# Idle-time identity products on the tensor engine, and a new order of the first loads, in a fused attention and expert kernel

## The chip, the cores and the metric

The kernel runs on one core of one Trainium2 chip. The metric is the device time of one execution in microseconds (us). Before the change it is 997.39 us, the median of three runs.

The core has five engines that run their own instruction queues: PE (the tensor engine), DVE (vector), ACT (scalar), POOL (GpSimd) and SP, which here only issues DMAs. ACT issues a few DMAs too. An instruction waits on semaphores for work of other engines; behind it on its own engine everything waits with it.

## The reference

Top-k style attention (scores within `tau` of the row's maximum survive) feeds a mixture of four experts. Sizes: 4 batches, 8 heads, 576 positions of 64; the 2304 x 512 result goes through experts with 1024 hidden units each.

```
scores = scale * q @ k.T                       # (4, 8, 576, 576)
thresh = max(scores, -1) - tau
scores = where(scores >= thresh, scores, -1e9)
attn   = softmax(scores)
x      = (attn @ v)  as (2304, 512)
p      = domain_probs / sum(domain_probs)
out    = sum over e of  p[:, e] * (relu(x @ w1[e]) @ w2[e])
```

All inputs are float32.

## The kernel before

The kernel describes its work as operations with an engine, a guessed duration, the tiles that they use, and a priority. `Plan.schedule` then runs a list scheduler over them: it walks a model of the five engines in time, and whenever an engine is free it takes the ready operation of lowest priority number. `Plan.emit` issues the instructions in the order that came out. So a change in a guessed time can move instructions on every engine; the durations themselves are not used by the chip. `Plan.clock` stretches the guessed duration of a PE operation when the model believes the tensor engine's clock to be low.

Heads are treated in pairs. The first batch (b = 0) runs in float32, the other three with split float16 operands. For a pair of heads in the first batch:

- `t_load` loads q and k (four DMAs of 128 KB, the first 512 positions); `tails` loads the last 64 positions of all heads of the batch into one tile `tl` (two 64 KB DMAs of k, one 128 KB DMA of q);
- `t_prep` transposes q and k on PE against the identity `ident` into the PSUM tile S (or its twin S0 for odd pairs): eight transposes of `raw` (line 628), two of `tl` (632, 633). ACT copies the result to T (647);
- `item` makes scores: `emit_qk` (919, 925) writes S in PSUM, DVE reads it into SS and takes the row extreme (978, two instructions, one per head), ACT takes the exponential (1001), DVE masks it and sums (1010); PE transposes E into ET (1030, 1059), ACT copies to PT (941);
- `group` multiplies with v (PE `av`, 1242 and 1251), spreads the row sums over columns (PE `rp`, 1206; ACT `rb`, 1226), multiplies the two on DVE (1273) and splits the result into two float16 halves X (ACT 1287, DVE 1295).

Then come the experts. `unit` does experts 0 and 1 while attention still runs (first layer 1358, second layer 1400, `mm` tiles in PSUM; ACT makes `hr` and `h`, 1370 and 1378); `unit7` does experts 2 and 3 afterwards (1594, 1674). Weights are scaled and split first (ACT 453 squares, PE 463 sums into S, then ACT 826 and DVE 851).

[...] Columns 0 to 575 and 960 to 1535 hold scores; between them lie two small places `am0` and `am1` for the sums of line 463.

DMA issues of SP and ACT share eight completion semaphores (`DMAHW0` to `DMAHW7`), which are handed out round the list; a DMA that takes a semaphore over waits at issue until the one before on it has landed.

Of the kernel before, what the change touches and what calls it, by code (L numbers as in the profile page):

```python
# [21 lines left out]
class Plan:  # L22
# [14 lines left out]
    GAP, FILL = 400, 3000  # L37
    WINDOW, WARMUP = 3413.0, 4000.0
    warm, cold, work, window, pe_end = True, 0.0, 1e9, 0, 0.0
    FREED, LANES = 55, 8  # L40
    START, DONE, HELD = 625, 1000, 877

    def __init__(self):
        self.ops, self.writer, self.readers = [], {}, {}
        self.slots, self.kinds, self.order, self.users = {}, {}, {}, {}
        self.tiles, self.loose = {}, set()
# [39 lines left out]
    def clock(self, now, ns, use):  # L86
        if use[0][0] != "mm" and self.warm:
            return ns
        self.warm = False
        w = int(now / self.WINDOW)  # L90
        if w != self.window:
            if self.work < 0.4 * self.WINDOW or w > self.window + 1:
                self.cold = self.WARMUP
            self.window, self.work = w, 0.0
        if now - self.pe_end > 300 and self.cold > 0:
            self.cold = self.WARMUP
        if self.cold > 0:
            slow = min(ns, self.cold / 2)
            self.cold -= 2 * slow
            ns += slow  # L100
        self.work += ns
        self.pe_end = now + ns
        return ns

    def schedule(self):
# [21 lines left out]
        starts, self.plan = [], {}  # L127
# [19 lines left out]
        while True:  # L147
            progress = True
            while progress:
                progress = False  # L150
                for e in engines:
# [13 lines left out]
                    if pick is None:  # L165
                        continue
# [10 lines left out]
                    if e == "PE":  # L177
                        ns = self.clock(now, ns, use)
                    end = now + ns + (self.TAIL[e] if e == "PE" else 0)
                    free[e] = end - self.TAIL[e]  # L180
                    if xfer and e != "SP":
                        dma = max(dma, end + self.START) + xfer
                        end = dma + self.DONE
                    elif xfer:
                        dma = max(dma, end + self.START) + abs(xfer)
                        if xfer < 0:
                            free[e] = max(end, dma - min(self.HELD, 100 - xfer))
                        end = dma + self.DONE
                        lanes.append(end)
                        if len(lanes) >= self.LANES:  # L190
                            free[e] = max(free[e], lanes[-self.LANES] - 100)
# [8 lines left out]
            if what == 0:  # L200
                for u in self.ops[i][4]:
                    s = (self.kinds[u[0]][0], u)
                    left[s] -= 1
                    if not left[s]:
                        heapq.heappush(events, (now + self.FREED, 3, s))
                e = self.ops[i][0]
                for j in succ[i]:
                    lat = self.LAT.get((e, self.ops[j][0]), 60)
                    at[j] = max(at[j], now + lat)
                    need[j] -= 1  # L210
                    if not need[j]:
                        heapq.heappush(events, (at[j], 1, j))
# [5 lines left out]
        assert len(starts) == n, f"{n - len(starts)} ops cannot start"  # L218
# [18 lines left out]
def topk_attention_moe_kernel(  # L237
# [11 lines left out]
    nc = tc.nc  # L249
# [13 lines left out]
    pl = Plan()  # L263

# [96 lines left out]
    for i in range(2):  # L361
        pl.pool(f"am{i}", 1)
        pl.kind(f"am{i}", f"am{i}", lambda _, i=i: s_all[:, 704 + 128 * i:832 + 128 * i])
# [138 lines left out]
    def setup():  # L502
        load(lambda: tau_sb, lambda: tau.partition_broadcast(128), 20000, ["tau"], prio=-50)
# [43 lines left out]
    def tails(b, prio):  # L547
# [10 lines left out]
        for h in range(2):  # L558
# [8 lines left out]
            131072, [("tl", b, 2)], use=u, prio=prio,  # L567
# [1171 lines left out]
    with tc.manual_schedule():  # L1739
# [4 lines left out]

        gp(400, lambda: make_identity(nc, ident), (), ["ident"], prio=-60)
# [6 lines left out]
        tails(0, -41)  # L1752
# [150 lines left out]
```

## Time and profile before

| | |
|---|---|
| median of three runs | 997.39 us (996.52 to 998.43) |
| the profiled execution | 995.66 us |
| its span, first to last instruction | 993.9 us |
| PE busy | 947.5 us (95%) |
| DVE busy | 734.4 us (74%) |
| ACT busy | 558.4 us (56%) |

Outside the span the profiled execution has 1.8 us. PE's busy share says how little is idle over the whole; where its idle time lies is seen by stages.

### The profile page before, as it was taken

Reading aid. Unit: us, or ns where it says so; the run is one execution under the profiler, and the core shown is the slowest. Engines: PE = TensorE matmul, PEld = TensorE weight load, DVE = VectorE, ACT = ScalarE, POOL = GpSimd, SP = SyncE. Lnnn points to the kernel's source line nnn. Section 1 sums busy time; section 2 is a strip of 40 time slices with the busy share of each in tenths; the row PEclk is TensorE's granted clock in tenths of the full one; section 3 lists DMA queues with packets and bytes.
Section 4 is the critical chain, followed back from the end, with each engine's and each line's share of the span. In section 5 each row is a group of like instructions: output and inputs, shape, how many; then the busy total and the mean of one; then the engine's idle time right before and its main releaser. Section 6 shows DMA issues by size and latency. Waiting matters only on the chain.

```text
span 993.9 us, 20153 instructions
## 1 busy us (share of the span) xinstructions
PE 947.5 (95%) x7472; PEld 614.8 (62%) x7472; DVE 734.4 (74%) x1826; ACT 558.4 (56%) x1177; POOL 253.3 (25%) x401
## 2 busy tenths in 40 slices
PE   7689989999998999999999999999999999999998
PEld 4365655566555556665666666767666667666663
DVE  3788788999888998889964543897665588655551
ACT  3797787786777778776665658643122232322220
POOL 1235462454334345433442234100000000000000
PEclk9989999999999999999999999999999999999999
DMA  8802256965799868887663233111110202001001
GB/s 190 246 12 77 63 109 147 195 129 113 148 161 215 138 111 153 180 143 146 116 117 99 65 106 108 66 52 40 57 33 1 84 24 70 17 1 53 33 1 42
DMA packets 243234, 95.99 MB, mean 97 GB/s; under 512 B 209600, under 2 KB 230080, under 8 KB 243136
## 3 DMA queue, kind: packets, MB, share of 16 engines
q1 hardware_dynamic: 241024, 94.18, 42.7%
q8 instruction: 58, 0.95, 0.4%
q10 hardware_dynamic: 2112, 0.52, 0.3%
q14 instruction: 40, 0.33, 0.1%
HBM read 40.41 MB, written 14.16 MB: 55 GB/s over the span
## 4 chain that ended last, share of the span: by engine, by line
PE 58%; DVE 15%; DMA 8%; ACT 6%; issue 4%; SPq 1%; POOL 0%; DVEq 0%; ACTq 0%
PE mm L1674 17%; PE Q L1594 16%; PE mm L1400 9%; PE mm L1358 9%; DMA PT<-E 6%; DVE SS L978 3%; DVE E L1010 3%; PE S L919 3%; PE av L1242 2%; DVE E L1135 2%; DMA wraw<-in_moe_w_dram 1%; ACT hr L1370 1%; ACT E L1129 1%; DVE wraw L1487 1%; PE S L925 1%
## 5 line engine op out<-in xcount | busy, mean ns | idle before, releaser
L1674 PE MATMUL mm<-WP,h 128*128 128x512 f16 x864 | 221.7, 379 | 0.0
L1400 PE MATMUL mm<-W,h 128*128 128x512 f16 x864 | 206.9, 379 | 1.0 <-ACT hr L1370 0.9
L1358 PEld LDWEIGHTS <-W 128*128 128x128 f16 x2016 | 174.7, 98 | 37.4 <-issue 7.6
L1594 PEld LDWEIGHTS <-WP 128*128 128x128 f16 x1680 | 153.7, 98 | 65.0 <-issue 1.6
L1358 PE MATMUL mm<-X,W 128*128 128x256 f16 (+1 forms) x1632 | 183.0, 267 | 5.3 <-ACT hr L1370 4.8
L1635 ACT ACTIVATE h<-qt 128x256 f16<-128x256 f32 (+1 forms) x160 | 62.2, 395 | 221.4 <-DVE qt L1614 221.2
L1614 DVE SCALAR_TENSOR_TENSOR qt<-Q,wc,qt 128x256 f32<-128x256 f32 (+1 forms) x280 | 124.5, 454 | 61.6 <-PE Q L1594 57.6
L1385 POOL TENSOR_TENSOR h<-hr,h 128x256 f16<-128x256 f32 (+1 forms) x168 | 131.6, 789 | 127.8 <-ACT h L1378 108.9
L1001 ACT ACTIVATE E<-SS,sm 128x576 f32<-128x576 f32 x144 | 109.8, 771 | 45.6 <-DVE SS L978 26.1
L1010 DVE SCALAR_TENSOR_TENSOR E<-SS,sm,E 128x576 f32<-128x576 f32 x144 | 123.2, 866 | 11.6 <-ACT E L1001 8.7
L1400 PEld LDWEIGHTS <-h 128*128 128x128 f16 x864 | 81.8, 99 | 77.0 <-issue 2.7
L1594 PE MATMUL Q<-T,WP 128*128 128x256 f16 (+1 forms) x960 | 117.5, 262 | 0.2 <-DVE qt L1614 0.2
L1674 PEld LDWEIGHTS <-h 128*128 128x128 f16 x864 | 82.8, 98 | 54.9
L993 POOL TENSOR_SCALAR sm<-sm,tau_p 128x1 f32<-128x1 f32 x144 | 67.2, 467 | 179.6 <-DVE SS L978 116.3
L1135 DVE SCALAR_TENSOR_TENSOR E<-E,ri,E 128x576 f16<-128x576 f32 (+1 forms) x120 | 93.0, 803 | 10.8 <-ACT E L1129 9.8
L1129 ACT ACTIVATE E<-E,ri 128x576 f16<-128x576 f32 (+1 forms) x120 | 83.5, 723 | 20.4 <-DMA PT<-E 9.0
L978 DVE TENSOR_SCALAR_CACHE_REDUCE SS<-S,qc 128x576 f32<-128x576 f32 x108 | 85.9, 808 | 8.3 <-DMA PT<-E 5.1
L1594 PE MATMUL Q<-X,WP 128*128 128x256 f16 (+1 forms) x720 | 89.0, 262 | 0.2
L1370 ACT ACTIVATE hr<-mm,wc 128x256 f32<-128x256 f32 (+1 forms) x168 | 72.1, 434 | 27.8 <-PE mm L1358 25.1
L1642 DVE SCALAR_TENSOR_TENSOR h<-qt,h 128x256 f16<-128x256 f32 (+1 forms) x160 | 61.6, 395 | 29.6 <-ACT h L1635 26.8
L1551 POOL TENSOR_SCALAR psc<-pnv,wpm 128x2 f32<-128x2 f32 (+1 forms) x20 | 6.9, 348 | 298.9 <-DVE acc L1692 275.9
L919 PE MATMUL S<-T 64*128 64x512 f16 (+3 forms) x440 | 74.7, 439 | 8.4 <-DVE SS L978 8.2
(145 smaller groups left out, 1003.9 us busy)
## 6 DMA issues: line engine op xcount, KB each, us to landing
wraw<-in_moe_w_dram SPq DMA_DIRECT2D x64, 256.0 KB, 3.9
part<-acc SPq DMA_DIRECT2D x18, 256.0 KB, 2.6
X<-x_dram SPq DMA_DIRECT2D x9, 512.0 KB, 3.5
acc<-part SPq DMA_DIRECT2D x18, 256.0 KB, 3.4
raw<-in_q_dram SPq DMA_DIRECT2D x32, 128.0 KB, 2.9
out_dram<-acc SPq DMA_DIRECT2D x16, 256.0 KB, 2.3
raw<-in_k_dram SPq DMA_DIRECT2D x28, 128.0 KB, 3.0
x_dram<-X SPq DMA_DIRECT2D x7, 512.0 KB, 3.3
```

Source lines behind the costliest of these rows:

```text
L919: nc.tensor.matmul(ps[:, 1024 * h:1024 * h + SM] if j < 4 else ps[rows(h), 0:SM], qm(h, a), km(h, c), start=(y == 0), stop=(y == last),)
L978: nc.vector.tensor_scalar(out=pl.t(*ssu)[:, S * h:S * h + S], in0=pl.t(*su)[:, 960 * h:960 * h + S], scalar1=qc[:, g, 2:3] if g >= NP * T3 ...
L1001: lambda h=h: nc.scalar.activation(out=pl.t(*eu)[:, S * h:S * h + S], in_=pl.t(*ssu)[:, S * h:S * h + S], func=ACTF.Exp, scale=-1.0, bias= ...
L1010: lambda h=h, col=col: nc.vector.scalar_tensor_tensor(out=pl.t(*eu)[:, S * h:S * h + S], in0=pl.t(*ssu)[:, S * h:S * h + S], scalar=pl.t(* ...
L1129: nc.scalar.activation(out=o, in_=e, func=ACTF.Copy, scale=pl.t(*ru)[:, h:h + 1])
L1135: nc.vector.scalar_tensor_tensor(out=o, in0=e, scalar=pl.t(*ru)[:, h:h + 1], in1=hh, op0=ALU.mult, op1=ALU.subtract,)
L1358: nc.tensor.matmul(ps[:, 0:n], w[:, wp, 0, c * 128:(c + 1) * 128], x[:, c, xp, c0:c0 + n], start=(i == 0), stop=(i == len(seq) - 1),)
L1385: lambda hu=hu, hru=hru: nc.gpsimd.tensor_tensor(out=pl.t(*hu)[:, 1, 0:n], in0=pl.t(*hru)[:, 0:n], in1=pl.t(*hu)[:, 0, 0:n], op=ALU.subtra ...
L1400: nc.tensor.matmul(ps, h[:, hp, 128 * i:128 * i + 128], w[:, wp, 1, :], start=(f == f0 and hp == 0 and wp == 0), stop=(f == f1 - 1 and hp ...
L1594: nc.tensor.matmul(reg(r), w[:, wp, o:o + 128], xb(b, c, xp), start=(n == 0), stop=(n == 5),)
L1614: lambda: nc.vector.scalar_tensor_tensor(out=tmp(o), in0=reg(r), scalar=wcs, in1=tmp(i), op0=ALU.mult, op1=ALU.add),
L1674: nc.tensor.matmul(ps, ht()[:, hp, 128 * i:128 * i + 128], w[:, wp, o:o + 512], start=(f == 0 and hp == 0 and wp == 0), stop=(f == NF - 1 ...
```

## The change

Three things are edited.

1. **Fill products.** Where the scheduler finds PE free and nothing ready, early in the program, it now inserts four matmuls of the float16 identity with itself (`idle`, line 1768 of the changed kernel). They write columns 832 to 959 of S, which no one reads; `am0` and `am1` shrink from 128 to 64 columns to make room.
2. **The first loads.** The q tails of batch 0 go by ACT's DMA queue, all tails of batch 0 get a priority ahead of the q and k loads of the first pair, and `tau` goes behind both.
3. **The scheduler's model.** `clock` is rewritten: it starts at the low clock and follows it by stretches of time. A DMA that transposes is guessed 400 ns longer (`LATE`). `SLACK` is added with only zeros, so it changes nothing.

```diff
-    def clock(self, now, ns, use):
-        if use[0][0] != "mm" and self.warm:
-            return ns
...
+    def clock(self, now, ns):
+        w = int((now - self.PHASE) // self.WINDOW)
+        while self.window < w:
...
                     if pick is None:
+                        if e == "PE" and self.fill and self.fill[0] <= now < self.fill[1] and (
+                            len(starts) < n + fills and self.busy(now) < self.KEEP * self.WINDOW
+                        ):
...
+                            self.ops.append(("PE", ns, self.fill[2], set(), (), 0.0, 0))
...
+                        if xfer < 0:
+                            end += self.LATE
...
+    pl.LATE = 400
...
-        pl.kind(f"am{i}", f"am{i}", lambda _, i=i: s_all[:, 704 + 128 * i:832 + 128 * i])
+        pl.kind(f"am{i}", f"am{i}", lambda _, i=i: s_all[:, 704 + 64 * i:768 + 64 * i])
...
-        load(lambda: tau_sb, lambda: tau.partition_broadcast(128), 20000, ["tau"], prio=-50)
+        load(lambda: tau_sb, lambda: tau.partition_broadcast(128), 20000, ["tau"], prio=-40.5)
...
-            131072, [("tl", b, 2)], use=u, prio=prio,
+            131072, [("tl", b, 2)], use=u, prio=prio, by="ACT" if b < 1 else "SP",
...
+        def idle():
+            for _ in range(4):
+                nc.tensor.matmul(s_all[:, 832:960], ident16, ident16, start=True, stop=True)
+
+        if 0.8:
+            pl.KEEP, pl.fill = 0.8, (1400, 140000, idle)
...
-        tails(0, -41)
+        tails(0, -41 if 1 == 0 else -43)
```

The rows below are the built programs' own. In them `x2` means two equal rows, and [waits ...] names the semaphores; line numbers of the changed kernel are 23 to 29 higher in the parts shown.

SP's DMA issues at the start of the program, before (`raw_182` is the first pair of heads, `raw_196` the second, `raw_209` the third):

```order
L434 DMA tau_sb<-in_tau_dram 128x1
L434 DMA raw_182<-in_q_dram 128x4x64 x2
L434 DMA tl<-in_k_dram 64x4x64
L434 DMA tl<-in_k_dram 64x4x64 [waits DMAHW0_49]
L434 DMA tl<-in_q_dram 64x8x64 [waits DMAHW1_49]
L434 DMA raw_196<-in_q_dram 128x4x64 [waits DMAHW2_49]
L434 DMA raw_196<-in_q_dram 128x4x64 [waits DMAHW3_49]
```

And SP's of the changed kernel at the same place (`raw_189` is now the first pair, `raw_203` the second):

```order
L457 DMA tl<-in_k_dram 64x4x64 x2
L457 DMA raw_189<-in_q_dram 128x4x64 x2
L457 DMA tau_sb<-in_tau_dram 128x1 [waits DMAHW1_49]
L457 DMA raw_203<-in_q_dram 128x4x64 [waits DMAHW2_49]
L457 DMA raw_203<-in_q_dram 128x4x64 [waits DMAHW3_49]
```

The k tails moved from behind the first pair's q to the head, `tau` from the head to behind them with a wait for the first k tail, and the q tails left SP's queue.

ACT's queue at the start of the changed kernel; before it held the four k loads of the first two pairs without a wait, and then the table load:

```order
L457 DMA tl<-in_q_dram 64x8x64
L457 DMA raw_189<-in_k_dram 128x4x64 x2
L457 DMA raw_203<-in_k_dram 128x4x64
L457 DMA raw_203<-in_k_dram 128x4x64 [waits DMAHW0_49]
L670 ACT_TABLE_LOAD
```

The q tails stand first, and the second pair's last k load now waits until they have landed.

PE, the program's first stretch without much ready, before: the sum for v (463), the first `av`, and what follows up to the sixth scores:

```order
L463 MATMUL S<-st,ones 128x4
L1030 MATMUL ET<-ident,E 128x128 x8
L919 MATMUL S<-T 128x512 x2
L925 MATMUL S<-T 128x2x64
L1059 MATMUL ET<-ident,E 128x128
```

PE of the changed kernel from the same sum on. Between the sum and the scores stand 24 fill products, of which the 9th and the 21st wait for DVE; the 21st is shown:

```order
L486 MATMUL S<-st,ones 128x4 [waits DVE_49,Pool_49]
...
L1770 LDWEIGHTS ident_166
L1770 MATMUL S<-ident_166 128x128 [waits DVE_49]
...
L942 MATMUL S<-T 128x512 x2
L948 MATMUL S<-T 128x2x64
L1053 MATMUL ET<-ident,E 128x128 [waits Activation_49]
L1053 MATMUL ET<-ident,E 128x128 x3
L1053 MATMUL ET<-ident,E 128x128 [waits DVE_49,PE_49]
L1053 MATMUL ET<-ident,E 128x128 x3
```

The scores (919, now 942) stand ahead of the eight transposes into ET instead of behind them.

In all, 228 fill products stand in the changed program: 48 ahead of the first transpose, 8 between the first and the second pair's transposes, and 172 in groups of 4 to 32 from there to the first expert products, the last of them among the first of these. Nine places in the 172 carry a wait for a reader of S (DVE, once ACT). Behind the first layer's start PE's order differs from before in many places by an operation or two: of the 884,736 columns that the products of experts 0 and 1 stream, at most 7,680 more or fewer stand ahead of any one set of scores than before.

## Rows read from the trace of the kernel before

**Rows 1.** The page's first part: engine, busy us (share of the span), instructions.

```profile
PE 947.5 (95%) x7472; PEld 614.8 (62%) x7472; DVE 734.4 (74%) x1826; ACT 558.4 (56%) x1177; POOL 253.3 (25%) x401
```

**Rows 2.** Stages by windows: length, busy us of each engine, granted clock, DMA share.

```profile
0.00:65.00 65.00, 44.87 (x266) 28.03 (x266) 41.62 (x132) 42.31 (x74) 15.67 (x34) 0.92 0.67 171
65.00:520.00 455.00, 434.60 (x3772) 274.76 (x3770) 403.08 (x1038) 347.05 (x727) 195.08 (x296) 1.00 0.69 134
520.00:993.90 473.90, 468.07 (x3438) 312.05 (x3436) 289.73 (x657) 168.99 (x377) 42.60 (x71) 1.00 0.16 50
```

**Rows 3.** The first stage in finer windows; the same columns.

```profile
5.00:20.00 15.00, 12.69 (x44) 7.60 (x45) 3.43 (x9) 4.98 (x8) 1.30 (x3) 1.00 0.91 188
10.00:62.00 52.00, 39.97 (x245) 25.01 (x245) 37.95 (x126) 37.78 (x69) 12.50 (x23) 0.90 0.66 178
50.00:60.00 10.00, 7.89 (x63) 6.54 (x64) 8.20 (x28) 8.05 (x17) 3.13 (x3) 0.66 0.01 2
```

**Rows 4.** Timeline, 0 to 19 us: start, us, engine, line, what [idle before <- releaser].

```profile
1.18 1.36 SPq L434 DMA_DIRECT2D raw<-in_q_dram  x2
1.33 0.29 DVE L1748 CAST ident<-ident 128x128 f16<-128x128 f32 x1 [1.33 <-POOL ident masks.py:199]
4.68 0.62 SPq L434 DMA_DIRECT2D tl<-in_q_dram  x1
6.11 1.94 PE L628 MATMUL S<-ident,raw 128*128 128x128 f32 x8 [6.11 <-DMA raw<-in_q_dram]
8.95 0.36 PE L632 MATMUL S<-ident,tl 64*128 64x64 f32 x1 [0.91 <-DMA tl<-in_q_dram]
9.90 1.94 PE L628 MATMUL S<-ident,raw 128*128 128x128 f32 x8 [0.19 <-DMA raw<-in_q_dram]
12.47 2.08 PE L919 MATMUL S<-T 64*128 64x512 f32 x4
15.42 0.82 DVE L978 TENSOR_SCALAR_CACHE_REDUCE SS<-S,qs 128x576 f32<-128x576 f32 x1 [11.54 <-PE S L925]
18.14 0.82 DVE L978 TENSOR_SCALAR_CACHE_REDUCE SS<-S,qs 128x576 f32<-128x576 f32 x1 [1.15 <-PE S L925]
```

**Rows 5.** Timeline of PE, 22 to 28 us, the same kinds of work.

```profile
22.58 1.04 PE L628 MATMUL S<-ident,raw 128*128 128x128 f32 x8
23.75 0.33 PE L633 MATMUL S<-ident,tl 128*128 128x128 f32 x1
26.27 1.13 PE L919 MATMUL S<-T 64*128 64x512 f32 x4
27.33 0.49 PE L925 MATMUL S<-T 128*128 128x128 f32 x2
```

**Rows 6.** Timeline, 34 to 40 us, DVE and PE around the sixth scores.

```profile
34.46 0.81 DVE L978 TENSOR_SCALAR_CACHE_REDUCE SS<-S,qs 128x576 f32<-128x576 f32 x1
35.22 1.69 PE L1030 MATMUL ET<-ident,E 128*128 128x128 f32 x8 [3.46 <-ACT rb L1226]
36.83 2.08 PE L919 MATMUL S<-T 64*128 64x512 f32 x4
39.41 0.82 DVE L978 TENSOR_SCALAR_CACHE_REDUCE SS<-S,qs 128x576 f32<-128x576 f32 x1 [2.69 <-PE S L925]
```

**Rows 7.** Timeline, 56 to 70 us: PE at both paces, and DVE's wait.

```profile
56.07 0.43 PE L1206 MATMUL rp<-ident,r 128*64 128x128 f16 x4 [0.49 <-ACT PT L941]
56.24 1.97 PE L1242 MATMUL av<-PT,V 128*64 128x128 f32 x16
58.98 0.29 DVE L1273 TENSOR_TENSOR x<-av,rb 128x128 f32<-128x128 f32 x1 [1.19 <-PE av L1251]
65.78 1.09 PE L1242 MATMUL av<-PT,V 128*64 128x128 f32 x16
67.67 1.50 PE L1358 MATMUL mm<-X,W 128*128 128x128 f16 x24
```

**Rows 8.** Waits of PE from 60 us on: who for whom, us in total, times, longest.

```profile
PE av L1242 <- DMA PT<-E: 4.7, 6, 1.7
```

More of the change, by code (lines that the diff above doesn't have):

```diff
@@ L36 @@
     TAIL = {"PE": 160, "ACT": 102, "DVE": 83, "POOL": 20, "SP": 0}
-    GAP, FILL = 400, 3000
-    WINDOW, WARMUP = 3413.0, 4000.0
-    warm, cold, work, window, pe_end = True, 0.0, 1e9, 0, 0.0
+    WINDOW, PHASE, LOW, HIGH = 3413.0, 1420.0, 0.58, 0.8
+    cold, work, window = True, 0.0, -1
+    KEEP, FILL, fill = 0.75, 220, None
     FREED, LANES = 55, 8
+    SLACK, LATE = {}, 0
     START, DONE, HELD = 625, 1000, 877
@@ L45, in __init__ @@
         self.slots, self.kinds, self.order, self.users = {}, {}, {}, {}
-        self.tiles, self.loose = {}, set()
+        self.tiles, self.loose, self.past = {}, set(), []
     def pool(self, name, n):
@@ L84, in reserve, with busy @@
         return s
-    def clock(self, now, ns, use):
-        if use[0][0] != "mm" and self.warm:
-            return ns
[L89 to L100, printed above, removed]
+    def clock(self, now, ns):
+        w = int((now - self.PHASE) // self.WINDOW)
+        while self.window < w:
+            if self.work < self.LOW * self.WINDOW:
+                self.cold = True
+            elif self.work > self.HIGH * self.WINDOW:
+                self.cold = False
+            self.window += 1
+            self.work = 0.0
+        if self.cold:
+            ns += min(ns, self.PHASE + (w + 1) * self.WINDOW - now)
         self.work += ns
-        self.pe_end = now + ns
         return ns
+    def busy(self, now):
+        h = self.past
+        while h and h[0][1] < now - self.WINDOW:
+            h.pop(0)
+        return sum(e - max(s, now - self.WINDOW) for s, e in h)
     def schedule(self):
@@ L126, in schedule @@
                 heapq.heappush(ready[o[0]], (o[5], i))
-        starts, self.plan = [], {}
+        starts, self.plan, fills = [], {}, 0
         def can(use):
@@ L165, in schedule @@
                     if pick is None:
+                        if e == "PE" and self.fill and self.fill[0] <= now < self.fill[1] and (
+                            len(starts) < n + fills and self.busy(now) < self.KEEP * self.WINDOW
+                        ):
+                            progress = True
+                            fills += 1
+                            ns = self.clock(now, self.FILL)
+                            self.past.append((now, now + ns))
+                            free[e] = now + ns
+                            heapq.heappush(events, (free[e], 2, -1))
+                            starts.append((now, seq, len(self.ops)))
+                            self.ops.append(("PE", ns, self.fill[2], set(), (), 0.0, 0))
+                            seq += 1
                         continue
@@ L177, in schedule @@
                     if e == "PE":
-                        ns = self.clock(now, ns, use)
+                        ns = self.clock(now, ns)
+                        self.past.append((now, now + ns))
                     end = now + ns + (self.TAIL[e] if e == "PE" else 0)
@@ L204, in schedule @@
                     if not left[s]:
-                        heapq.heappush(events, (now + self.FREED, 3, s))
+                        heapq.heappush(events, (now + self.FREED + self.SLACK.get(s[0], 0), 3, s))
                 e = self.ops[i][0]
@@ L208, in schedule @@
                     lat = self.LAT.get((e, self.ops[j][0]), 60)
+                    if e != "PE" and e != self.ops[j][0]:
+                        lat += self.SLACK.get(self.ops[j][0], 0)
                     at[j] = max(at[j], now + lat)
@@ L217, in schedule @@
                 heapq.heappush(ready[o[0]], (o[5], i))
-        assert len(starts) == n, f"{n - len(starts)} ops cannot start"
+        assert len(starts) == n + fills, f"{n + fills - len(starts)} ops cannot start"
+        self.fills = fills
         self.end = now
@@ L263, in topk_attention_moe_kernel @@
     pl = Plan()
+    pl.SLACK = {"PE": 0, "DVE": 0, "ACT": 0,
+                "s": 0, "b": 0, "ma": 0, "mm": 0, "q": 0}
+    pl.LATE = 400
     first = ctx.enter_context(ExitStack())
```

## The prediction

> **What bounds the kernel now.** I read the busy shares first: PE is busy 95% of the span, no other engine above 74% [rows 1]. The windows by stage then show where the other 46 us of PE lie [rows 2]: 20.1 of the first 65 us are idle, 20.4 of the next 455, and 5.8 of the last 474. So from about 65 us on PE sets the pace, and what ends the first stretch earlier should end the program earlier by as much, as long as later waits stay as they are. In the first 65 us PE waits: it has little to do until the first expert products, and the work goes round from PE to DVE to ACT and back.
>
> Then the clock. [...] From 5 to 20 us the column reads 1.00, but the durations say otherwise: eight transposes of raw take 1.94 us at 6.11 and at 9.90, and 1.04 us at 22.58; a set of score products takes 2.08 at 12.47 and 1.13 at 26.27 [rows 4, 5]. I trust the durations: until about 18 us PE runs at the low level, and what is recorded as 1.00 is the lack of a record. So the stretch that the change is aimed at does exist. [...]
>
> **The sum, step by step.** It is made against the profiled execution, 995.66 us (span 993.9 and 1.8 around it); the median of the three runs is 1.7 us higher, and I take the gain off that.
>
> *Head.* Before, the q of the first pair is issued by 2.54 and PE can begin at 6.11, 3.57 later; the q tails are issued at 4.68, land last, and stop PE again until 8.95 [rows 4]. After, two k tails go ahead of q on SP, each about as long to issue as the q tails' 0.62, so q is issued by 2.54 + 1.24 = 3.8 at the latest (tau no longer stands ahead of it) and lands by 7.3; the tails are there by then. The 48 fill products start when the identity is cast, 1.62. One costs 62.5 ns at the high level (24 expert products of the same width in 1.50 us) and at most 107 ns at the low one (4 spread products in 0.43) [rows 7]: they end between 4.6 and 6.8, under the cover of that load. Without the cover they would cost up to 5.1 us. The first pair's transposes then take 1.50 us at the high level (22.58 to 24.08) [rows 5] and end at 8.8. Eight more fills follow, 0.5 us, and ACT's first copy waits for them, but the second pair's q does not come before 9.9 [rows 4], and I add 0.3, since its issue now waits for k loads that ACT issues 0.6 later. From 10.2: 1.50 for the second pair, 1.55 for the first scores (26.27 to 27.82) [rows 5], 0.15 to DVE: DVE's first reading starts at 13.4 in place of 15.42. The second scores are then ready as the first readings end, so DVE's 1.15 us wait before 18.14 goes as well. Together 3.1 us. At the low level throughout nothing is gained, and the 0.3 is lost; that is the lower bound. I take 3.0, because the fills are dense and the rows nearest in kind, at 22.58, are at the high level.
>
> The later landing of tau costs nothing: only DVE's constants wait for it, and DVE has nothing before 13.4. The ACT queue stands still until the q tails have landed (about 5), behind it one k load and the table load; the first copy is wanted after 8.8, so that is covered too.
>
> *Order at the sixth scores.* Before, PE waits 3.46 us for ACT with eight transposes at the head of its queue, then runs them in 1.69, and only then the scores, so DVE goes from one reading that ends at 35.27 to the next at 39.41, 4.14 us later, 2.69 of them in wait for these scores [rows 6]. After, the scores stand ahead of the transposes and need only S, which DVE has read. DVE still has to do X in between, which waits for ACT's rb, a weight square that now stands between, and ACT's half of X; I count some 2.8 us for that chain by the present gaps. Gain 1.3, between 0 and 2.1 (scores in 1.55 and nothing else).
>
> *Low level at 50 to 60 us.* The av products take 1.97 against 1.09 later, and DVE waits 1.19 for them [rows 7]. Fills stand ahead of this place in the program. Gain 1.1, or 0.
>
> *The fills' own cost.* 172 fills at 62.5 ns are 10.75 us of PE. PE's idle time from 10 to 62 us is 52 - 39.97 = 12.0 us [rows 3], so they nearly fit, but not everywhere: a group of four (0.25 us) that stands where the next operand is already there is late by 0.25. I charge four such groups, 1.0 us; bounds 0 and 10.75.
>
> *The later order.* The list is redone throughout. The 400 ns that the scheduler adds to transposing DMAs can remove at most PE's 4.7 us of waits for PT [rows 8], and as much can be lost the other way. Few columns change place and they go both ways: I take 0.
>
> Sum: 3.0 + 1.3 + 1.1 - 1.0 = 4.4 us. From the median that is 997.4 - 4.4 = **993.0 us** (991.3 for a profile as quick as the present one).
>
> **The rivals.**
>
> *No change.* The fills heat the clock but the level is lost again, or never reached in time: PE's first real work is 2.5 us of fp32 transposes with waits between. Then the head brings -0.3, the 50 us stretch 0, the order still 1.3, the fills still cost 1.0: 997.4 within 0.1. For it speaks that before, the scores at 12.47 were still at the low level with PE at work since 9.90 [rows 4]; against it, that transposes did run at the high level at 22.58, although between score products [rows 5]. [...]
>
> *More.* If DVE's waits of the first stretch all go (2.69 of [rows 6], 1.15 of [rows 4], 1.19 of [rows 7]), with the 2.0 by which its first reading comes earlier, that is 7.0 us; with half of the PT waits of [rows 8], 2.3, and 1.0 off for the fills it is 8.3: 989 us.
>
> *Slower: fills that hold PE for a reader of S.* The order shows nine fill places that wait for DVE's or ACT's reading of S, although they write columns that nobody reads, and what stands behind them on PE (spread products, the next transposes) waits too. If each held PE for one reading (0.82 us) [rows 4] and its own 0.25, that is 9.6 us; less the gains of 5.4 it is 4.2 us slower, 1001.6. It decides from five of the nine on, and only if DVE or ACT then waits for PE. For it: DVE is busy 37.95 of the 52 us from 10 to 62 [rows 3], so a wait for DVE can be long. Against it: what stands behind most of them needs the same reading anyway (the next scores into S). [...]
>
> **How the numbers follow.** A run of this kernel tells a change from none at about 0.2%, 2 us: faster is below 995.4, slower above 999.4. The forecast (990.5 to 995.4) gets 0.48; more than that (down to 986 and a little below) 0.20; no change (995.4 to 999.4), where the first stretch gains and the later order gives it back, or the clock stays low, 0.18; slower 0.14. So faster 0.68, same 0.18, slower 0.14. The range 986 to 998.5 leaves out the slower cases and slivers at both ends, some 0.18. The forecast's own range is 990.5 to 995.4.
>
> **What would show it.** The fills' rows must end before the first transpose starts, at about 7; raw transposes of the second pair must take about 1.0 and not 1.9 us; DVE's first reading at 13.4, and no DVE wait of over 2 us near 36; the granted clock 1.00 between 20 and 65 us; the first expert products some 4 us earlier than now; and a like lead at 520 us. The prediction is wrong if the lead is there at 65 us and gone at 520 (the later order), if PE rows show fills with DVE as releaser of their idle time and DVE waiting behind them, or if the transposes keep to 1.94.

## The result and the profile after

The changed kernel takes **986.54 us** (median of 4 runs, 984.57 to 989.59) against 997.2 for the kernel before in the same session (4 runs, 996.52 to 998.43). The ratio is 0.9894, 95% interval 0.9865 to 0.9924: faster by 10.7 us, where 4.4 were forecast. The profiled execution takes 987.71 us (span 985.9).

The page's first part, in the columns of [rows 1], and the same three stages as in [rows 2]:

```profile
PE 953.7 (97%) x7700; PEld 623.8 (63%) x7700; DVE 733.5 (74%) x1826; ACT 558.2 (57%) x1177; POOL 254.6 (26%) x401
```

```profile
0.00:65.00 65.00, 54.90 (x530) 40.61 (x530) 44.22 (x139) 45.16 (x79) 14.71 (x33) 0.95 0.64 171
65.00:520.00 455.00, 438.08 (x3792) 274.75 (x3791) 400.57 (x1035) 346.49 (x728) 199.02 (x297) 1.00 0.69 136
520.00:985.90 465.90, 460.70 (x3384) 308.41 (x3381) 288.70 (x653) 166.60 (x371) 40.90 (x71) 1.00 0.16 50
```

PE's idle time is 10.1, 16.9 and 5.2 us; it was 20.1, 20.4 and 5.8. But idle time turned into fills is no gain, so a ledger is needed. The group of all fills, from the costliest groups by line (busy us, mean ns of one, then the idle time ahead of them and its releasers):

```profile
L1770 PE MATMUL S<-ident 128*128 128x128 f16 x228 | 19.2, 242 | 7.0 <-DVE SS L1001 4.8 <-DVE ident L1777 1.7 <-ACT T L670 0.3
```

The span is PE's other work, plus fills, plus idle: 947.5 + 0 + 46.4 = 993.9 before, 934.5 + 19.2 + 32.2 = 985.9 after. Of the 19.2 us of fills 14.2 lie in former idle time, and the same other work takes 13.0 less. Work that runs at the high level instead of the low one is part of that (a set of eight transposes in 1.06 us instead of 1.94, in the rows below); how much of the 13.0 it is was not added up. Net 8.0.

The head, from the timeline of 0 to 15 us, answers to [rows 4]:

```profile
1.68 5.30 PE L1770 MATMUL S<-ident 128*128 128x128 f16 x48 [1.68 <-DVE ident L1777]
2.43 1.36 SPq L457 DMA_DIRECT2D raw<-in_q_dram  x2
8.04 1.06 PE L651 MATMUL S<-ident,raw 128*128 128x128 f32 x8 [1.05 <-DMA raw<-in_q_dram]
9.40 0.61 PE L1770 MATMUL S<-ident 128*128 128x128 f16 x8
9.85 1.07 PE L651 MATMUL S<-ident,raw 128*128 128x128 f32 x8
11.33 1.13 PE L942 MATMUL S<-T 64*128 64x512 f32 x4
13.03 0.82 DVE L1001 TENSOR_SCALAR_CACHE_REDUCE SS<-S,qs 128x576 f32<-128x576 f32 x1 [3.83 <-PE S L948]
14.51 0.81 DVE L1001 TENSOR_SCALAR_CACHE_REDUCE SS<-S,qs 128x576 f32<-128x576 f32 x1
```

The fills end at 6.98 under cover of the load, the sets of transposes take 1.06 and 1.07 instead of 1.94, the scores 1.13 instead of 2.08, and DVE's first reading starts at 13.03 instead of 15.42. Its third follows without a wait, at 14.51 instead of 18.14.

The place of [rows 6], from the timeline of 30 to 39 us:

```profile
30.72 1.12 PE L1770 MATMUL S<-ident 128*128 128x128 f16 x12 [1.48 <-DVE SS L1001]
31.89 0.82 DVE L1001 TENSOR_SCALAR_CACHE_REDUCE SS<-S,qs 128x576 f32<-128x576 f32 x1 [0.35 <-PE S L1770]
32.77 0.58 PE L1770 MATMUL S<-ident 128*128 128x128 f16 x4 [0.92 <-DVE SS L1001]
33.28 2.08 PE L942 MATMUL S<-T 64*128 64x512 f32 x4
...
35.87 1.91 PE L1053 MATMUL ET<-ident,E 128*128 128x128 f32 x8
36.12 0.82 DVE L1001 TENSOR_SCALAR_CACHE_REDUCE SS<-S,qs 128x576 f32<-128x576 f32 x1 [0.94 <-PE S L948]
```

The scores are at the low level here (2.08), as they were before [rows 6]. In windows, with the stretch of [rows 3] beside it:

```profile
31.00:38.00 7.00, 6.08 (x30) 4.17 (x28) 3.64 (x13) 6.10 (x13) 1.71 (x4) 0.51 0.82 230
...
50.00:60.00 10.00, 8.78 (x107) 6.86 (x106) 8.41 (x33) 8.87 (x17) 0.83 (x2) 1.00 0.00 0
```

And before, from 20 to 40 us:

```profile
20.00:40.00 20.00, 14.77 (x91) 8.49 (x89) 15.97 (x55) 13.23 (x27) 4.06 (x11) 0.91 0.97 289
```

So the level that was partly low at 50 to 60 is now high there, and the low stretch around the sixth scores, which was there before, has grown, with fills standing in it. An estimate from the granted clocks of these windows and of [rows 3] (taken as a mix of 1.00 and of 0.50, which the repeat of this kernel shows from 8 to 11 us, so that the low level takes twice the share that is missing): some 3.6 us at the low level from 20 to 40 and 6.8 from 50 to 60 before, 6.9 from 31 to 38 after.

What the fills did just ahead of the first expert products (after, timeline of 53 to 59 us):

```profile
54.22 0.36 ACT L1249 ACTIVATE rb<-rp,v_c 128x128 f32<-128x128 f32 x1
55.22 1.05 PE L1770 MATMUL S<-ident 128*128 128x128 f16 x16 [0.92 <-DVE SS L1001]
56.21 1.09 PE L1265 MATMUL av<-PT,V 128*64 128x128 f32 x16
57.74 0.29 DVE L1296 TENSOR_TENSOR x<-av,rb 128x128 f32<-128x128 f32 x1 [0.94 <-PE av L1274]
```

The av products are at the high level, 1.09 instead of the 1.97 of [rows 7]. But sixteen fills ahead of them wait 0.92 us for a reading of S and then run for 1.05, so that av starts 1.6 us after ACT's rb is done, and DVE waits 0.94 us for it, against 1.19 before.

Where does the lead arise? One line's own view gives the first and last start of its products. The first expert products (L1381) and the first products of the second layer (L1617), after:

```profile
L1381 PE MATMUL mm<-X,W x1632: 219/272/283, 58.8 to 606.2; 128*128 128x256 f16 x160, 128*128 128x128 f16 x22
...
L1617 PE MATMUL Q<-T,WP x960: 217/272/273, 624.3 to 959.6; 128*128 128x256 f16 x153, 128*128 128x128 f16 x39
```

and before:

```profile
L1358 PE MATMUL mm<-X,W x1632: 217/273/421, 60.0 to 614.1; 128*128 128x256 f16 x160, 128*128 128x128 f16 x22
...
L1594 PE MATMUL Q<-T,WP x960: 216/272/273, 632.3 to 967.6; 128*128 128x256 f16 x153, 128*128 128x128 f16 x39
```

The first expert products come 1.2 us earlier, the second layer 8.0 us earlier. (By 65 us DVE has also done 2.6 us more of its work than before; the first stage is therefore worth 1 to 3 us.) Most of the lead arises between 60 and 624 us, where the forecast had put nothing. One place of it can be named. PE's timeline of before at 126 to 136 us:

```profile
126.65 1.47 PE L1358 MATMUL mm<-X,W 128*128 128x256 f16 x12
131.78 2.72 PE L1358 MATMUL mm<-X,W 128*128 128x256 f16 x12 [3.66 <-ACT hr L1370]
```

PE waits 3.66 us for ACT's hr, and the twelve products behind the wait take 1.25 us more than the twelve ahead of it. In the new list PE waits for no hr at all. That alone does not make the gain: in none of the other remade lists (experiment 6) does PE wait longer than 2.1 us for an hr, and two of those are no faster than before. PE's waits from 60 us on, after, to be read against [rows 8]:

```profile
PE S L942 <- DVE SS L1001: 8.7, 9, 1.7
PE av L1265 <- DMA PT<-E: 4.0, 5, 1.7
```

The wait for PT, which the "More" rival wanted halved, is 0.7 us shorter only.

### The profile page after: what moved, and what is told of

Same layout as the page of the kernel before. It is cut to its first block, busy times and chain, and to the rows that moved or that the text cites. A ratio compares the mean times of both kernels' runs of the same rounds, so it can differ in the third digit from the quotient of the medians.

```text
span 985.9 us, 20613 instructions
## 1 busy us (share of the span) xinstructions
PE 953.7 (97%) x7700; PEld 623.8 (63%) x7700; DVE 733.5 (74%) x1826; ACT 558.2 (57%) x1177; POOL 254.6 (26%) x401
## 4 chain that ended last, share of the span: by engine, by line
PE 67%; DVE 12%; DMA 8%; ACT 6%; issue 4%; SPq 2%; POOL 1%; ACTq 0%; DVEq 0%; POOLq 0%
PE mm L1697 17%; PE Q L1617 16%; PE mm L1423 12%; PE mm L1381 10%; DMA PT<-E 4%; PE S L942 4%; PE av L1265 3%; SPq L457 2%; DVE E L1033 2%; DVE SS L1001 2%; DVE E L1158 2%; DMA wraw<-in_moe_w_dram 2%; DMA T<-R 1%; ACT E L1024 1%; ACT E L1152 1%
## 5 line engine op out<-in xcount | busy, mean ns | idle before, releaser
L1617 PEld LDWEIGHTS <-WP 128*128 128x128 f16 x1680 | 153.7, 98 | 65.1 <-issue 1.6
L1381 PEld LDWEIGHTS <-W 128*128 128x128 f16 x2016 | 174.1, 98 | 29.6 <-issue 0.4
L1381 PE MATMUL mm<-X,W 128*128 128x256 f16 (+1 forms) x1632 | 181.1, 266 | 0.0
L1617 PE MATMUL Q<-T,WP 128*128 128x256 f16 (+1 forms) x960 | 117.5, 262 | 0.2 <-DVE qt L1637 0.2
L1016 POOL TENSOR_SCALAR sm<-sm,tau_p 128x1 f32<-128x1 f32 x144 | 71.2, 495 | 174.9 <-DVE SS L1001 103.3
L1617 PE MATMUL Q<-X,WP 128*128 128x256 f16 (+1 forms) x720 | 88.9, 262 | 0.2
```

The costliest lines, as they stand in the source:

```text
L1381: nc.tensor.matmul(ps[:, 0:n], w[:, wp, 0, c * 128:(c + 1) * 128], x[:, c, xp, c0:c0 + n], start=(i == 0), stop=(i == len(seq) - 1),)
L1617: nc.tensor.matmul(reg(r), w[:, wp, o:o + 128], xb(b, c, xp), start=(n == 0), stop=(n == 5),)
```

## The experiments

One theory: the gain is the lifted clock of the head plus, by chance, a remade list with fewer waits later. Its rivals: the loads make the head; the new model makes the list better in itself; the later fills earn their time by holding the clock. Experiments 1 to 5 and 7 keep the order of the changed kernel on PE, DVE and ACT, fills aside; the four of experiment 6 have the list made anew. The results stand together in the table, for the profile and the medians; "reading" is DVE's first reading of scores, "expert" and "second" the first products of the two layers, all in us of the profiled execution. That execution need not be a typical one: for "no fills", "loads swapped" and "model only" it is the longest of the kernel's runs, for "first 56, again" the shortest.

| kernel | median (runs) | ratio, 95% | profiled | reading | expert | second |
|---|---|---|---|---|---|---|
| before | 997.2 (4) | | 995.66 | 15.42 | 60.0 | 632.3 |
| after | 986.54 (4) | 0.9894 [0.9865, 0.9924] | 987.71 | 13.03 | 58.8 | 624.3 |
| after, again | 987.56 (6) | 0.9895 [0.9874, 0.9916] | 987.83 | 14.47 | 58.5 | 624.5 |
| no fills | 992.28 (10) | 0.9957 [0.9938, 0.9975] | 995.81 | 16.07 | 59.5 | 632.5 |
| first 56 alone | 984.50 (4) | 0.9888 [0.9849, 0.9927] | 983.57 | 12.91 | 56.6 | 620.2 |
| first 56, again | 985.98 (6) | 0.9883 [0.9862, 0.9904] | 982.37 | 12.88 | 54.7 | 619.0 |
| later 172 alone | 988.87 (4) | 0.9928 [0.9903, 0.9952] | 988.29 | 14.53 | 60.2 | 624.9 |
| eight a place | 991.52 (10) | 0.9954 [0.9937, 0.9972] | 991.43 | 14.32 | 64.2 | 627.7 |
| first 72 + 8 alone | 983.58 (6) | 0.9866 [0.9842, 0.9890] | 983.61 | 13.31 | 55.5 | 620.3 |
| loads swapped | 990.25 (6) | 0.9923 [0.9900, 0.9947] | 992.52 | 13.28 | 58.9 | 629.2 |
| old loads, new list | 999.62 (10) | 1.0030 [1.0011, 1.0050] | 1002.27 | 13.28 | 62.2 | 638.9 |
| LATE 0, new list | 993.51 (10) | 0.9965 [0.9947, 0.9983] | 992.71 | 14.39 | 58.4 | 629.3 |
| model only, new list | 990.16 (6) | 0.9927 [0.9902, 0.9952] | 992.65 | 15.68 | 57.7 | 629.3 |
| loads only, new list | 997.72 (10) | 1.0009 [0.9991, 1.0028] | 996.44 | 15.15 | 58.9 | 633.1 |

Each ratio is to the kernel before in the same session. Its median was 997.2 us beside "after", 996.73 beside "no fills", the first "first 56 alone", "later 172 alone" and "old loads", 996.58 beside both repeats, "eight a place" and "loads swapped", and 997.66 beside the other four. The last three sessions ran on different chips.

**1. No fills.** The fill places stay in the list and issue nothing.

```diff
         def idle():
-            for _ in range(4):
-                nc.tensor.matmul(s_all[:, 832:960], ident16, ident16, start=True, stop=True)
+            pass
```

> The changed kernel with the same order on every engine, but the 228 fill products are not issued. Clock theory (the fills lift the tensor engine's clock early, and that is worth the head's 2 to 3 us and about 1 us near 55): raw transposes at about 1.9 us again, DVE's first reading near 15.3, time 989.5 to 992, between the two kernels. Order theory (the new order alone makes the gain): within 1.5 us of the changed kernel's 986.5. Cost theory (the fills hold PE more than they give): faster than the changed kernel, 984.

992.28, 0.3 above what the clock theory gave: the order and the loads alone are worth 4.4 us against 996.73, the fills the other 5 to 6. The head is at the low level as before (1.94 and 1.91 for a set of transposes), and later (16.07, where 15.3 was expected), since q comes about 2 us later (timeline, 0 to 20 us):

```profile
8.14 1.94 PE L651 MATMUL S<-ident,raw 128*128 128x128 f32 x8 [8.14 <-DMA raw<-in_q_dram]
10.58 1.91 PE L651 MATMUL S<-ident,raw 128*128 128x128 f32 x8
16.07 0.82 DVE L1001 TENSOR_SCALAR_CACHE_REDUCE SS<-S,qs 128x576 f32<-128x576 f32 x1 [6.98 <-PE S L948]
```

The profiled execution is this kernel's longest of ten, 3.5 us over the median; its granted clock over the whole span is the lowest of the ten, 0.987 (the others 0.990 to 0.996), and it is 0.94 from 65 to 140 us, where the changed kernel has 1.00 all the way to 520.

**2. The first 56 alone,** run twice (the second time beside the changed kernel), and **3. the later 172 alone.**

```diff
+        calls = []
         def idle():
-            for _ in range(4):
+            calls.append(0)
+            for _ in range(4 if len(calls) <= 14 else 0):
```

(For the later ones the condition is turned round.)

> Only the first 56 fill products are issued (48 ahead of the first transposes, 8 behind them); order as in the changed kernel. Clock theory: head as in the changed kernel (DVE's first reading near 13.0), but PE at the low level somewhere between 35 and 60 us; time 987 to 989. If the later fills only cost: 985 to 986. If the first fills do nothing: as without fills.

> Only the later 172 fill products are issued, order as in the changed kernel. Clock theory: head as before (first reading near 15.3), no low level from 40 to 60 us; 988 to 990. If the later fills are pure cost: slower than the kernel without any fills by 1 to 3 us.

> The first 56 products alone once more (the other 172 left out, everything else in the order of the changed kernel). Theory A, that the gain lies in lifting the clock before the first transposes and in the remade list, and that the later 172 cost more PE time than they give back: 983 to 986 us, 1 to 3 below the changed kernel of the same call, although the level falls to the low one more often before 55 us. Theory B, that the 2 us seen in the first such run were chance and that holding the clock pays for the later fills: the same as the changed kernel or 1 to 3 us above it, 988 to 990.

> The changed kernel once more, unaltered, so that the three kernels beside it are compared with it on the same chip. Both theories: 985 to 990 us, a profile near 987.7 with the first fills at 1.68, the first transposes in 1.06 at 8.0 and DVE's first reading at 13.0.

The first 56 alone take off 7.8 us from the kernel without fills (984.50, under either theory's range), the later 172 alone 3.4, both together 5 to 6: beside the first ones, the later ones seem to take time. Against the changed kernel the first ones alone are 2.0 us faster by the first two medians, which come from different sessions, and 1.6 by the second two, from one session. By the ratios to before it is 0.6 and 1.2 us. The ranges and the intervals overlap, so the direction is likely but not shown, and the size is open. The traces lean the same way: the first expert products stand at 56.6 and 54.7 us against 58.8 and 58.5. The first 65 us of the first such run, as windows:

```profile
0.00:65.00 65.00, 50.55 (x368) 34.31 (x368) 46.06 (x145) 45.99 (x85) 15.92 (x35) 0.87 0.70 171
```

and its fills by line:

```profile
L1773 PE MATMUL S<-ident 128*128 128x128 f16 x56 | 5.6, 289 | 1.7 <-DVE ident L1780 1.7
```

The granted clock is lower, 0.87 against 0.95, yet DVE has done 46.06 us of work against 44.22 (in the second run 47.90, at 0.95). Ahead of the first expert products, where sixteen fills held av back, av now starts as soon as ACT's rb is done (second run, timeline of 49 to 55 us):

```profile
52.26 1.09 PE L1265 MATMUL av<-PT,V 128*64 128x128 f32 x16 [1.00 <-ACT rb L1249]
```

By the ledger the first of these runs has 941.7 of other work, 5.6 of fills and 34.5 of idle time: the later 172 (13.6 us of PE) save 7.2 us of other work and 2.3 of idle time.

The 7.8 us are more than the head shows: DVE's first reading moves by 3.2 (16.07 to 12.91), the first expert products by 2.9, and in the profiles another 9.4 arises up to the second layer (573.0 without fills, 563.6 with the first 56), with the order the same. Two rows of the kernel without fills name most of it, PE's wait for PT from 60 us on and the window 65 to 140:

```profile
PE av L1265 <- DMA PT<-E: 6.4, 8, 1.3
```

```profile
65.00:140.00 75.00, 70.49 (x585) 44.88 (x586) 60.25 (x167) 58.35 (x140) 41.80 (x54) 0.94 0.32 74
```

With the first 56 PE waits 2.1 us for PT, and the window has 1.00. The low clock of the window is some 4.5 us, by an estimate from 75 us and 0.06, and belongs to an execution that was 3.5 us over its median; how often it comes without fills isn't known. But a lead of 3 us need not pass through as 3 us: here later waits differ although no instruction changes place, so the shares of "list" and "fills" can't be told apart by a difference of medians alone.

**4. Eight a place.** `range(8)` in `idle`, all 57 places.

> Eight products at each of the 57 fill places instead of four, everything else in its order. Theory A, that fills cost PE time where they are not under cover: the first 96 run at the low level to about 7.2 and end near 10.0 (45 more at 62.5 ns), 2 us after the q that they wait beside, so DVE's first reading is at 15; of the other 172 added products (10.75 us) as large a share is lost as of the first 172, 2 to 4 us; together 4 to 6 us above the changed kernel, 991 to 994. Theory B, that PE has room for them everywhere and that the held clock pays: the low level at 31 to 38 goes, the head still loses 2, and the time is 986 to 989. A third way: each added group holds back DVE's next reading by its full 0.25 us, and the time is 997 or more.

991.52, 4.0 above the changed kernel of the same session, as the first theory had it; the ranges do not touch (990.37 to 996.04 against 984.17 to 988.17). The windows of its first stage and the waits of DVE:

```profile
0.00:65.00 65.00, 56.94 (x642) 44.56 (x643) 39.24 (x128) 40.48 (x71) 14.18 (x31) 1.00 0.69 168
```

```profile
DVE SS L1001 <- PE S L1770: 5.2, 5, 1.9
```

From the first transposes on (eight in 1.04 us) the clock is held, 1.00, and the stage is slower: DVE has done 39.24 us of work, 5.0 less than in the changed kernel, and waits 5.2 us for fills in all where it waited 1.3. In the head the 96 products end near 9.0, 1 us after q lands in the changed kernel, and DVE reads first at 14.32. In this stage the work goes round between PE, DVE and ACT, and the added fills cost more here than the low stretch that they remove.

**5. The loads swapped.** The places that the ten first load issues have in the finished list are given to them in the old sequence, and the q tails go by SP; nothing else moves.

```diff
-        for i in self.schedule():
+        order = self.schedule()
+        keys = [("rawqk", 0, 1, 0), ("rawqk", 0, 1, 1), "tau", ("rawqk", 0, 0, 0),
+                ("rawqk", 0, 0, 1), ("tl", 0, 0), ("tl", 0, 1), ("tl", 0, 2)]
+        ids = [self.writer[k] for k in keys]
+        places = sorted(order.index(i) for i in ids)
+        for p, i in zip(places, ids):
+            order[p] = i
+        for i in order:
```

> The changed kernel with its first loads alone put back: tau first on SP, then q, the k tails and the q tails on SP, nothing ahead of k on ACT; every other instruction stands on its engine where it stood. Theory A, that the loads move the head by a few tenths only (q is issued 1.7 - 0.6 = 1 us earlier, the q tails land about 1.5 us later and stop PE once): DVE's first reading at 12.8 to 13.4 against 13.03, time within 1 us of the changed kernel, 986 to 989. Theory B, that the loads are what makes the head earlier, the stall for the q tails (0.4 to 0.9 us) giving the clock time to fall: first reading at 14 to 15.4, second transposes at 1.5 to 1.9 instead of 1.07, time 2 to 3 us above the changed kernel.

Its head (timeline, 5 to 14 us):

```profile
6.22 1.06 PE L658 MATMUL S<-ident,raw 128*128 128x128 f32 x8 [0.30 <-DMA raw<-in_q_dram]
9.12 0.27 PE L662 MATMUL S<-ident,tl 64*128 64x64 f32 x1 [1.83 <-DMA tl<-in_q_dram]
13.28 0.82 DVE L1008 TENSOR_SCALAR_CACHE_REDUCE SS<-S,qs 128x576 f32<-128x576 f32 x1 [9.35 <-PE S L955]
```

The first q comes 1.8 us earlier, the q tails stop PE for 1.83, and the first reading is 0.25 later than in the changed kernel; the first expert products stand within 0.1. So in the head the new loads are worth a few tenths, as the first theory had it. The time, 990.25, is the second theory's all the same, 2.7 above the changed kernel, though the ranges overlap (986.24 to 992.52 against 984.17 to 988.17). In the profile, the longest of the six runs, this comes behind 240 us, with one low stretch near 290 (granted clock 0.83 from 285 to 295) and 1.2 us more of waits for PT. How loads of the first 10 us should reach there isn't shown; it stays open whether this is their doing or the spread of executions.

**6. Lists made anew.** Four kernels change what the planner is given: the loads of before under the new model with fills (204 of them; `tau` at -50, tails at -41, q tails on SP); `LATE = 0`; the new model with the loads of before and without fills; and the new loads alone under the old model. For the first and the second:

```diff
-        load(lambda: tau_sb, lambda: tau.partition_broadcast(128), 20000, ["tau"], prio=-40.5)
+        load(lambda: tau_sb, lambda: tau.partition_broadcast(128), 20000, ["tau"], prio=-50)
...
-            131072, [("tl", b, 2)], use=u, prio=prio, by="ACT" if b < 1 else "SP",
+            131072, [("tl", b, 2)], use=u, prio=prio,
...
-        tails(0, -41 if 1 == 0 else -43)
+        tails(0, -41)
```

```diff
-    pl.LATE = 400
+    pl.LATE = 0
```

> The changed kernel with the first loads as before (tau first, tails behind the first pair's q, the q tails on SP); the list is made anew, with 204 fills. If the loads matter (they let the first pair be transposed without a stop): first reading 0.5 to 1 us later than 13.0 and 987 to 988. If the second pair's q bounds the head anyway: first reading within 0.3 us, 985.5 to 987.5. Beyond that a difference comes from the changed order.

> The changed kernel with LATE = 0, the list made anew from it. Theory A, that some 4 us of the gain are the remade list and that this part hangs on where a remade list happens to leave its waits: the first 30 us are those of the changed kernel (DVE's first reading at 13.0 to 14.5), and the time may be anywhere from 985 to 1000, the difference lying behind 65 us. Theory B, that the 400 ns for transposing DMAs are what the later gain is: PE's waits for PT come back (6.9 us and more, against 4.0), and the time is 989 to 992. Theory C, that the later list is worth nothing: within 1 us of 987.5.

> The new planner model (clock, LATE) with the loads of before and no fill: one part of the change alone. Theory A, the remade list as chance: a head like that of before (first reading at 15 to 16), and 990 to 1002 according to the later waits. Theory B, that the new model makes a better list in itself: 992 to 994, 3 to 4 us under before, as the changed list without its fills was (992.3), with the long wait for hr near 130 us gone.

> The kernel before with the three edits of the loads alone, the list made anew by the old model. In the head q lands about 1 us later and the q tails some 1.5 us earlier, at the low level: first reading at 15.4 to 16.3, so -0.5 to +0.9 us there. Theory A, the remade list as chance: 990 to 1003, set behind 65 us. Theory B, that the loads bring something of their own: 994 to 996.

By the order in their traces any two of these lists, the changed one and that of before differ by at least 130 of ACT's instructions and 150 of DVE's. The times are 999.62, 993.51, 990.16 and 997.72. The first was expected at 985.5 to 988 by either theory. The loads of before under the new model have a good head (reading 13.28) and lose it all later; PE's waits there, from 60 us on:

```profile
PE S L942 <- DVE SS L1001: 12.1, 16, 1.8
PE AM L486 <- ACT junk L476: 5.4, 3, 3.4
```

In the other direction the model alone has the head of before (15.68) and still gains 7.5 us. That `LATE` makes the later gain has something for it: without it PE waits 8.3 us for PT instead of 4.0, the first expert products stand 0.4 us earlier and the second layer 5.0 later. (Against the repeat of the changed kernel, which has the same head within 0.1 us, it is 4.8 later.) But the list with old loads has the same `LATE`, waits for PT only 2.9 us, and is the slowest of all. From the first expert products to the second layer the five remade lists, before included, take 570.9 to 576.7 us in their profiles, the changed list 563.5 to 566.0 in seven of its nine profiled kernels and 570.3 and 573.0 in the other two, the swapped loads and the kernel without fills. So the list of the changed kernel is worth some 4 us by the medians without fills, and in seven profiles with fills 6 to 9, each against the one profile of before. Whether it is a good draw or the new model makes better lists isn't settled: the two lists of the old model take about 997 and 998 us, and of the four of the new model three are faster than that and one, with the old loads, is slower. No single input of the planner was shown to be the cause.

**7. More of the first, none of the later.** Six products at each of the first twelve places, four at the next two, none afterwards.

```diff
-            for _ in range(4):
+            calls.append(0)
+            for _ in range(6 if len(calls) <= 12 else 4 if len(calls) <= 14 else 0):
```

> The first fills alone, 72 products instead of 48 ahead of the first transposes, then 8, and none later; the order of the changed kernel otherwise. Theory A, that the gap between the last fill and the landing of q (1 to 2 us) lets the level fall in some executions, as in the repeat of the changed kernel, where the transposes took 1.94 at 8.06 after fills that ended at 5.8: with 72 they end at 7.3 to 8.5, the transposes are at the high level in the profile, and the time is 983 to 986, up to 1 us under the 56 alone. Theory B, that the longer row of fills only puts the transposes off: first reading at 13.3 to 13.9, and 985 to 987.

```profile
1.68 6.83 PE L1773 MATMUL S<-ident 128*128 128x128 f16 x72 [1.68 <-DVE ident L1780]
8.34 1.04 PE L651 MATMUL S<-ident,raw 128*128 128x128 f32 x8
```

The fills end at 8.51, about when q has landed, the transposes are at the high level (1.04), and the time is the best of all, 983.58 (982.33 to 985.71); five of its six runs are below every run of the changed kernel, whose ten lie at 984.17 to 989.59, in other sessions. That 72 do better than 56 isn't shown (ratio intervals 0.9842 to 0.9890 and 0.9862 to 0.9904).

## Why the prediction came out as it did

Direction and range held, and the forecast's own range (990.5 to 995.4) did not: the time is that of the rival "More", but not by its mechanism, and terms were mis-sized in opposite directions. That 986.54 lies inside the stated range, half a microsecond above its lower end, is luck in so far as most of the gain came from where the sum had 0.

- **Head, +3.0.** The mechanism was right: 2.4 at the first reading, where 2.0 were forecast (2.5 with the first 56 alone), and 3.6 at the third, where DVE's wait is gone and 3.1 were forecast; 2.6 are left at the reading ahead of the sixth scores (31.89 against 34.46). q was issued by 3.79, as forecast, but landed 4.25 us after that instead of 3.57. In the repeat the first reading gained only 0.95, because the first transposes fell into the low level (1.94, last section). I took the 3.0 because the fills are dense, and no row of before shows that dense products lift the clock. What the runs show is the sets of transposes behind them: 1.06 and 1.07 with fills, 1.94 and 1.05 in the repeat, 1.94 and 1.91 without fills.
- **Loads at nothing for tau and a few tenths for the rest.** Right in the head (0.25); what the swap changed later is open.
- **Sixth scores, +1.3.** They stood earlier, and DVE's reading came at 36.12 instead of 39.41: 3.3, of which 2.6 stood ahead of it. So 0.7, within the bounds given. DVE's gap is 3.4 and not 2.8; the scores ran at the low level.
- **Low level at 50 to 60, +1.1.** It went from there (granted clock 1.00 instead of 0.66, av in 1.09 instead of 1.97), and DVE's wait for av fell by 0.25 only, from 1.19 to 0.94. The step that failed is that fills ahead of a place give it the faster clock for nothing: sixteen of them wait for DVE and then run in the time that av could have had. At 31 to 38 they did not hold the level either (granted clock 0.51); those at 30.72 and 32.77 wait 2.4 us for DVE's readings, while PE stands still. Twice as many held it there (1.00 over the first 65 us, the scores in 1.13 instead of 2.08), at a higher cost (experiment 4).
- **The fills' own cost, -1.0.** Too small in the first stage, and sized by the wrong thing. I charged PE time. The changed kernel's first expert products stand 2.2 to 3.8 us later than without the later 172, and DVE waits 1.3 us for fills outright. Their net cost beside the first 56 is 1.6 to 2.0 us by the medians and 0.6 to 1.2 by the ratios, and isn't clear of the spread.
- **The first stage together** therefore gave 1 to 3 us and not 4.4.
- **The later order, 0.** This is the term that failed by most. I took the few displaced columns of expert products as a sign of little change and looked at the waits for PT alone. The list without fills is 4.4 us faster than before, and in the profiles of before and after the stretch from the first expert products to the second layer is 6.8 us shorter (565.5 against 572.3); the wait of 3.66 for hr and the slow products behind it, 4.9 together, stood in the trace of before and were no term of mine. I also made it a condition that later waits stay as they are; in experiment 2 they differ with the order unchanged (6.4 against 2.1 us for PT). What in the list makes the gain stays open.

Of the signs named ahead, the rows of the fills, the transposes, the first reading and DVE's wait near 36 (0.94) came as said; the granted clock did not stay at 1.00 (0.51 from 31 to 38), the first expert products came 1.2 us earlier and not 4, and one sign of being wrong came in small: fills that wait for DVE, with DVE waiting behind them.

The rivals. *No change* needed the low level in the head: the transposes ran in 1.06, so it fell. *Slower by fills that hold PE for a reader of S*: the waits are there, 4.8 us on PE, and DVE waits 1.3 for fills outright, not 9.6; the doubled fills show the mechanism at four times that (5.2). At this size it takes from the gain and does not decide its sign.

## What to carry to other kernels

Here fill products paid ahead of the first operand, under cover of its load: 56 of them took 7.8 us off the kernel without fills. The 172 later ones took 3.4 off by themselves, beside the first ones they probably cost 1 to 2, and doubling all of them cost 4. So once work goes round between engines, set what a fill holds back against the clock that it holds, and measure the two kinds apart. When an edit makes a scheduler redo its list, the list is a change of its own, here from 7.5 us faster to 3 slower; compare the edit with the order kept. Even with the order kept, later waits can differ between a kernel that starts 3 us earlier and one that doesn't. A long wait in the profile of before, on the engine that bounds, deserves a line in the sum with its bounds, even where the diff doesn't touch it.

## What the hardware showed that was not expected

**The level's moments differ between executions of one program.** The same kernel, repeated (timeline, 1 to 16 us):

```profile
1.68 4.13 PE L1770 MATMUL S<-ident 128*128 128x128 f16 x48 [1.68 <-DVE ident L1777]
8.06 1.94 PE L651 MATMUL S<-ident,raw 128*128 128x128 f32 x8 [2.25 <-DMA raw<-in_q_dram]
11.29 1.05 PE L651 MATMUL S<-ident,raw 128*128 128x128 f32 x8
14.47 0.82 DVE L1001 TENSOR_SCALAR_CACHE_REDUCE SS<-S,qs 128x576 f32<-128x576 f32 x1 [5.60 <-PE S L948]
```

Its fills took 4.13 us and not 5.30, 86 ns a product and not 110, so the level rose sooner; PE then stood still for 2.25 us, and the transposes were at the low level again, granted clock 0.50 from 8 to 11 us. In exchange no low stretch followed (1.00 from 11.5 to 65), and the time was the same. The kernel with `LATE = 0`, which begins in the same way, did likewise: fills in 4.10 us, a stand of 2.18, transposes in 1.94, and a granted clock of 0.97 over the first 65 us in both. With stands of 1.05 (changed kernel, first run) and 0.30 (swapped loads) they took 1.06.

**The clock rose while PE ran nothing but transposes.** With the later 172 only, PE has run nothing but float32 transposes up to 12.4 us (timeline, 0 to 20 us):

```profile
10.07 0.37 PE L655 MATMUL S<-ident,tl 64*128 64x64 f32 x1
10.63 1.80 PE L651 MATMUL S<-ident,raw 128*128 128x128 f32 x8
12.37 0.28 PE L655 MATMUL S<-ident,tl 64*128 64x64 f32 x1
```

The transpose of a tail takes 0.37 at 10.07 and 0.28 at 12.37, the high level's time (0.27 in the changed kernel), and the scores behind it take 1.13. The rise is read from the durations alone: the granted clock is given as 1.00 from 8 to 12 us as well as from 12.2 to 14.5, as it is for the slow transposes of before [rows 3]. It is one execution: without fills the same transposes stayed at the low level (eight in 1.91 at 10.58).
